# Mamba-2 scan and PReLU feed-forward on one core: weight conversion two pieces ahead with its add on GpSimd, states kept unmasked, first decays spread earlier

## The chip, the cores and the metric

The kernel runs on 1 core of one Trainium2 chip. The metric is the device time of one execution, in microseconds (us); lower is better. A core has TensorE (PE in the profile, with its weight loads as PEld), VectorE (DVE), ScalarE (ACT), GpSimd (POOL) and SyncE (SP), which here only issues DMAs. Each engine works through its own instructions in order; they meet at semaphores.

## The reference

Two blocks follow each other. The first is a chunked state-space scan over 4 batches x 8 heads x 768 positions, head size 32, state size 16; the second a feed-forward block over the 3072 tokens, 256 -> 2048 -> 256, with a slope alpha for each hidden unit.

```python
log_a = np.log(np.clip(a, 1e-06, 1.0))
for c in range(nc):
    cum = np.cumsum(la, axis=-1)
    L = np.exp(cum[:, :, :, None] - cum[:, :, None, :]) * causal
    M = np.einsum('bhin,bhjn->bhij', Cc, Bc) * L
    y_intra = np.einsum('bhij,bhjd->bhid', M, xc)
    y_inter = np.einsum('bhin,bhnd->bhid', Cc, state) * np.exp(cum)[:, :, :, None]
    y[:, :, sl] = y_intra + y_inter
    state = decay_full * state + sum_j(Bc_j x_j * decay_from_j)
# (batch, head, seq, dim) -> (batch*seq, head*dim)
h = x @ w_in
out = (np.maximum(h, 0.0) + alpha * np.minimum(h, 0.0)) @ w_out
```

x, a, B and C are float32. w_in and w_out come as float64, 8 bytes a number, so the kernel has to turn them into float32 itself.

## The kernel before

**Scan.** The sequence is cut into 24 chunks of 128 positions (Q), two chunks at a time as a "pair" (`pair`, L264): pairs 0 to 11, three to a batch. `pair` is a Python generator, and each `ssm(gp)` emits its next stage, so the author places the stages by hand between the matmuls of the feed-forward block. The stages are: (1) `rows_prep` for pairs 0 and 6, clamps of the broadcast decays `abc` on POOL (L272), `bn` (B times the decay to the chunk's end) on POOL (L279), the prefix products `pf` on DVE (L285, L288), four transposes of B and C on PE (L296), and on ACT the copies `bh` and the four scaled `cz` (L300, L303); (2) the decay matrix `dec` of the first chunk, and `cd` (L325); (3) `dec` of the second chunk, then the chunk's contribution to the state: a matmul `dps` (L333), its product with the block mask `bmask` (`dm`, L335), and the running `state` (L345); (4), (5) for each chunk the products C*B on PE (L356), multiplied into `dec` on DVE (L361); (6) the output `y` on PE, from the state (L370) and from `dec` (L377), copied by ACT into `xT` (L383), the input of the feed-forward block.

`dec` is a scan over 1024 columns. For pairs 2 and up its input is `abc`, a DMA that broadcasts decays to all partitions (L115). For pairs 0 and 1 there is no such DMA: PE spreads the rows with 16 small matmuls a chunk (two PSUM tiles, L318), and DVE scans each tile of 512 columns (L322). The mask is needed because all 8 heads share the 128 state partitions: head h's 16 rows may only meet its own 32 columns.

**Weights.** 16 pieces of 512 KB (8 of w_in for two hidden blocks each, 8 of w_out for two blocks each). `load_weights` (L142) issues the DMA into one of six `raw` buffers. `convert_a` (L152) makes two parts on ACT (L163, L166). `convert` (L169) finishes on DVE: sign bits (L184, or L187 twice for w_out, with the sign of the slope), a clamp (L190), shift and xor (L192), and an integer add of the rounded low part (L195), which writes the piece into `w_in` or `w_out`.

**Feed-forward.** `hidden` (L390): two k-steps of matmuls into one of two PSUM buffers `hp` (L396), then ACT multiplies by the slope (L399) and DVE takes the larger or smaller of the two (L400). `output` (L403) runs 2 hidden blocks later (LAG) and accumulates into `po` (L409).

**Order.** PE, DVE and ACT run in the order in which the code emits (`manual_schedule`, L43); for POOL and SP a planner orders the instructions, so a load may be issued well before its place in the code. Token group 0 (512 tokens, pairs 0 and 1) is worked in two halves: n=0 runs 16 hidden blocks on pair 0's 256 tokens, n=1 on pair 1's, with outputs from f=2 on. The loop (L445) converts piece i+1 at odd f, right after `hidden(f)`, and loads piece i+6 at even f. `first` and `second` name the f at which stages of pairs 1, 2 and 3 are emitted. From group 1 on, blocks are 512 tokens wide and pair stages are placed at fixed f.

Of the kernel before, what the change touches and what calls it, by code (L numbers as in the profile page):

```python
# [9 lines left out]
F32 = mybir.dt.float32  # L10
U32 = mybir.dt.uint32
# [11 lines left out]
def kernel(  # L23
# [20 lines left out]
        mybir.EngineType.PE, mybir.EngineType.DVE, mybir.EngineType.Activation}))  # L44
# [3 lines left out]
    P = 128  # L48
# [120 lines left out]
    def convert(dst, src, sg):  # L169

        d = dst.bitcast(U32)
        sg = sg()
        if src.dtype == F32:
            for i in range(2 if sg else 0):
                nc.vector.tensor_scalar(out=d[:, i], in0=d[:, i], scalar1=sg[i], scalar2=None,
                                        op0=ALU.bitwise_xor)
            return
        hi, t, g = parts.pop(id(dst))  # L180
        tf = t.bitcast(F32)
        r = wtp.tile([P, 2, WQ], U32, name="wr")
        if sg is None:
            nc.vector.tensor_single_scalar(out=r, in_=hi, scalar=SIGN, op=ALU.bitwise_and)  # L184
        else:
            for i in range(2):
                nc.vector.tensor_scalar(out=r[:, i], in0=hi[:, i], scalar1=SIGN, scalar2=sg[i],  # L187
                                        op0=ALU.bitwise_and, op1=ALU.bitwise_xor)
# [6 lines left out]
        nc.vector.tensor_tensor(out=d, in0=r, in1=g.bitcast(U32), op=ALU.add)  # L195
# [25 lines left out]
    alp = ps_s.tile([P, 512], F32, name="ss")  # L221
    nc.tensor.transpose(alp[:, :NF], al_n, ident[:NF, :NF])
    over = const.tile([P, NF], F32, name="over")
    nc.vector.tensor_scalar(out=over, in0=alp[:, :NF], scalar1=1.0, scalar2=None, op0=ALU.is_gt)
    s_mul = const.tile([P, NF], F32, name="s_mul")
    nc.vector.tensor_scalar(out=s_mul, in0=over, scalar1=-2.0, scalar2=1.0, op0=ALU.mult,
                            op1=ALU.add)
    s_alpha = const.tile([P, NF], F32, name="s_alpha")
    nc.vector.tensor_tensor(out=s_alpha, in0=alp[:, :NF], in1=s_mul, op=ALU.mult)
    s_out = const.tile([P, NF], U32, name="s_out")  # L230
    nc.vector.tensor_single_scalar(out=s_out, in_=s_mul.bitcast(U32), scalar=SIGN,
                                   op=ALU.bitwise_and)
# [4 lines left out]

    prt = {}
    firsts = {}

    def rows_prep(i):
# [5 lines left out]
        if i == 0:  # L247
            z = prep.tile([RW, Q], F32, name="z0")
            nc.vector.tensor_scalar(out=z, in0=rows, scalar1=1e-6, scalar2=1.0,
                                    op0=ALU.max, op1=ALU.min)  # L250
            nc.vector.memset(z[:, :1], 0.0)
            firsts[0] = z
# [11 lines left out]
    def pair(gp):  # L264

        b, c = divmod(2 * gp, CPB)
        nat, abc, xt, ap = loads.pop(("p", gp))
        last = c + 2 == CPB
        if gp % 6 == 0:
            rows_prep(gp // 6)  # L270
        for t in abc:
# [10 lines left out]
            in1=pj.unsqueeze(3).to_broadcast([P, 2, H, N]), op=ALU.mult)  # L282

# [6 lines left out]


# [12 lines left out]
        cd = work.tile([P, 2, Q], F32, name="cd")  # L304
        yield


        dec = work.tile([P, 2, H, Q], F32, name="dec")
        dv = dec.rearrange("p k h t -> p k (h t)")
        for k in range(2):  # L310
            if abc:
                nc.vector.tensor_tensor_scan(out=dv[:, k], data0=abc[k], data1=ident_h,  # L312
                                             initial=0.0, op0=ALU.mult, op1=ALU.add)
            for w in range(0 if abc else 2):
                t = ps_s.tile([P, 512], F32, name="ss")
                for q in range(4):
                    row = (b % 2 * H + 4 * w + q) * CPB + c + k
                    nc.tensor.matmul(t[:, q * Q : (q + 1) * Q],  # L318
                                     ident[:RW, row : row + 1].to_broadcast([RW, P]), firsts[0],
                                     start=(q == 0), stop=True, skip_group_check=True)  # L320
                ws = slice(512 * w, 512 * w + 512)
                nc.vector.tensor_tensor_scan(out=dv[:, k, ws], data0=t, data1=ident_h[:, ws],  # L322
                                             initial=0.0, op0=ALU.mult, op1=ALU.add)
            if k == 0:
                nc.vector.tensor_tensor(out=cd.rearrange("p k t -> p (k t)"), in0=ct, in1=pf,  # L325
                                        op=ALU.mult)
                yield
# [4 lines left out]
        for k in range(nk):  # L332
            nc.tensor.matmul(dps[:, k * HD : (k + 1) * HD], bn[:, k], xt[:, k], start=True, stop=True)  # L333
        dm = work.tile([P, 2, HD], F32, name="dm")
        nc.vector.tensor_tensor(  # L335
            out=dm[:, :nk], in0=dps[:, : nk * HD].rearrange("p (k m) -> p k m", m=HD),
            in1=bmask.unsqueeze(1).to_broadcast([P, nk, HD]), op=ALU.mult)
        st = [state.get(b)]
        for k in range(nk):
            if st[k] is None:  # L340
                st.append(dm[:, k])
                continue
            new = work.tile([P, HD], F32, name=f"state{k}")
            e = (k + 1) * Q - 1
            nc.vector.scalar_tensor_tensor(out=new, in0=st[k], scalar=pf[:, e : e + 1],  # L345
                                           in1=dm[:, k], op0=ALU.mult, op1=ALU.add)
            st.append(new)
        state[b] = st[-1]
# [155 lines left out]
```

## Time and profile before

| | |
|---|---|
| median of 3 runs | 456.19 us (454.41 to 457.52) |
| the profiled execution | 456.93 us, span 455.2 us |
| PEld busy | 284.0 us (62%) |
| ACT busy | 124.3 us (27%) |
| POOL busy | 35.1 us (8%), 62 instructions |
| HBM read / written | 26.85 MB / 3.15 MB |

The span runs from the first to the last instruction of the profiled execution. "Busy" is the time in which an engine has an instruction running; matmuls are pipelined, and their ends are modelled. In the strips, each digit is the busy share of one of 40 equal slices, in tenths. An idle time is put down to whatever released the instruction that ended it, so a row `A <- B: 21.3, 8` says that A stood still 21.3 us in all, 8 times, until B was done.

### The profile page before, as it was taken

How to read it: one execution, taken by the hardware profiler on the slowest of the kernel's cores; microseconds unless marked ns; L12 is line 12 of the kernel's file. 1: busy time of each engine (PE TensorE's matmuls, PEld its weight loads, DVE VectorE, ACT ScalarE, POOL GpSimd, SP SyncE). 2: the span in 40 equal slices, each digit the busy share in tenths (PEclk: the TensorE clock that was granted, in tenths of full speed). 3: DMA queues.
4: the chain of work that ended last, by engine and by line, in shares of the span. 5: the costliest groups of instructions: out<-in, count | busy, mean ns of one | idle time of the engine just before them, and what ended most of it. 6: DMA issues, size and time to landing. Idle time of an engine off the chain costs nothing.

```text
span 455.2 us, 4968 instructions
## 1 busy us (share of the span) xinstructions
PE 421.7 (93%) x1931; PEld 284.0 (62%) x1931; DVE 230.6 (51%) x354; ACT 124.3 (27%) x229; POOL 35.1 (8%) x62
## 2 busy tenths in 40 slices
PE   3875755999999999999999999999999999999996
PEld 3564543787865665665765766666666666666664
DVE  4859676789575174283273273283283372122121
ACT  3133442543231231241231231311321311131121
POOL 2021002002001001012011021020010000000000
PEclk9959787999999999999999999999999999999999
DMA  9989473441151141161150170130020000010001
GB/s 176 240 219 177 120 170 110 117 79 47 24 121 54 23 88 40 23 135 40 24 120 7 24 170 3 24 93 1 0 94 0 0 1 0 1 47 0 1 0 46
DMA packets 105207, 30.31 MB, mean 67 GB/s; under 512 B 75792, under 2 KB 101088, under 8 KB 105184
## 3 DMA queue, kind: packets, MB, share of 16 engines
q1 hardware_dynamic: 101024, 29.74, 27.9%
q10 hardware_dynamic: 4160, 0.26, 0.7%
q8 instruction: 15, 0.25, 0.2%
q14 instruction: 8, 0.07, 0.0%
HBM read 26.85 MB, written 3.15 MB: 66 GB/s over the span
## 4 chain that ended last, share of the span: by engine, by line
PE 86%; DVE 9%; DMA 1%; ACT 1%; issue 1%; ACTq 0%; DVEq 0%
PE hp L396 37%; PE po L409 36%; PE ss L356 5%; PE ss L377 2%; PE ss L370 2%; PE ss L318 1%; PE ss L333 1%; DVE wr L192 1%; DMA nat<-in_C_dram 1%; DVE dec L322 1%; DVE gt L400 1%; DVE w_in L195 1%; DVE dec L312 1%; PE ss L296 1%; ACT gt L399 1%
## 5 line engine op out<-in xcount | busy, mean ns | idle before, releaser
L396 PE MATMUL hp<-xT,w_in 128*128 128x512 f32 (+1 forms) x448 | 192.4, 556 | 22.1 <-DVE w_in L195 21.3
L409 PE MATMUL po<-w_out,gt 128*128 128x256 f32 x768 | 181.1, 379 | 0.0
L409 PEld LDWEIGHTS po<-w_out,gt 128*128 128x128 f32 x768 | 145.9, 190 | 54.0 <-issue 38.3
L400 DVE SCALAR_TENSOR_TENSOR gt<-hp,s_mul,gt 128x512 f32<-128x512 f32 (+1 forms) x112 | 75.3, 673 | 186.9 <-ACT gt L399 186.0
L399 ACT ACTIVATE gt<-hp,s_alpha 128x512 f32<-128x512 f32 (+1 forms) x112 | 70.4, 629 | 263.7 <-PE hp L396 263.7
L396 PEld LDWEIGHTS hp<-xT,w_in 128*128 128x128 f32 x448 | 84.5, 198 | 89.3 <-issue 52.2
L312 DVE TENSOR_TENSOR_SCAN dec<-abc,ident_h 128x1024 f32<-128x1024 f32 x20 | 46.0, 2300 | 0.0
L361 DVE TENSOR_TENSOR dec<-ss,dec 128x512 f32<-128x512 f32 x48 | 30.8, 685 | 18.5 <-PE ss L356 18.5
L272 POOL TENSOR_SCALAR abc<-abc 128x1024 f32<-128x1024 f32 x20 | 21.3, 1066 | 180.4 <-DMA abc<-in_a_dram 118.2
L356 PE MATMUL ss<-cz,bh 64*128 64x512 f32 x96 | 29.4, 682 | 0.0
L303 ACT ACTIVATE cz<-ss,par 128x256 f32<-128x256 f32 x48 | 18.9, 482 | 0.0
L279 POOL TENSOR_TENSOR bn<-nat,prt 128x256 f32<-128x256 f32 x12 | 9.2, 773 | 120.4 <-PE ss L333 72.2
L383 ACT COPY xT<-ss 128x512 f32<-128x512 f32 x12 | 7.0, 586 | 36.3 <-PE ss L377 36.3
L356 PEld LDWEIGHTS ss<-cz,bh 64*128 64x128 f32 x96 | 7.9, 195 | 9.2 <-issue 7.6
L377 PE MATMUL ss<-dec,xt 128*32 128x128 f32 x384 | 13.3, 276 | 0.2 <-DVE dec L361 0.2
L322 DVE TENSOR_TENSOR_SCAN dec<-ss,ident_h 128x512 f32<-128x512 f32 x8 | 9.6, 1215 | 5.2 <-PE ss L318 5.2
L318 PEld LDWEIGHTS ss<-z,ident 96*128 96x128 f32 x64 | 11.4, 274 | 0.2
L192 DVE SCALAR_TENSOR_TENSOR wr<-wt,wr 128x512 uint32<-128x512 uint32 x16 | 11.1, 692 | 0.5
L318 PE MATMUL ss<-z,ident 96*128 96x128 f32 x64 | 11.3, 356 | 0.0
L333 PE MATMUL ss<-xt,bn 128*128 128x256 f32 x40 | 11.1, 392 | 0.0
L377 PEld LDWEIGHTS ss<-dec,xt 128*32 128x32 f32 x384 | 9.6, 109 | 2.1 <-DVE dec L361 0.6
L166 ACT ACTIVATE wg<-raw 128x512 f32<-128x512 uint16 x16 | 10.8, 674 | 0.0
(51 smaller groups left out, 142.5 us busy)
## 6 DMA issues: line engine op xcount, KB each, us to landing
abc<-in_a_dram SPq DMA_DIRECT2D x20, 512.0 KB, 3.7
raw<-in_moe_w_in_dram SPq DMA_DIRECT2D x8, 512.0 KB, 6.6
raw<-in_moe_w_out_dram SPq DMA_DIRECT2D x8, 512.0 KB, 3.4
xt<-in_x_dram SPq DMA_DIRECT2D x24, 128.0 KB, 3.8
out_dram<-o_sb SPq DMA_DIRECT2D x12, 256.0 KB, 2.6
ap<-in_a_dram SPq DMA_DIRECT2D x12, 128.0 KB
nat<-in_B_dram SPq DMA_DIRECT2D x22, 64.0 KB, 2.9
nat<-in_C_dram SPq DMA_DIRECT2D x22, 64.0 KB, 2.8
```

What stands on the lines that cost most here:

```text
L192: nc.vector.scalar_tensor_tensor(out=r, in0=t, scalar=3, in1=r, op0=ALU.logical_shift_left, op1=ALU.bitwise_xor)
L272: nc.gpsimd.tensor_scalar(out=t, in0=t, scalar1=1.0, scalar2=1e-6, op0=ALU.min, op1=ALU.max)
L303: nc.scalar.mul(cz[:, e].rearrange("p k t -> p (k t)"), ct, par[:, e : e + 1])
L312: nc.vector.tensor_tensor_scan(out=dv[:, k], data0=abc[k], data1=ident_h, initial=0.0, op0=ALU.mult, op1=ALU.add)
L318: nc.tensor.matmul(t[:, q * Q : (q + 1) * Q], ident[:RW, row : row + 1].to_broadcast([RW, P]), firsts[0], start=(q == 0), stop=True, skip_ ...
L356: nc.tensor.matmul(gram[r].rearrange("p h t -> p (h t)"), bh[rs, k], cz[rs, :, k], start=True, stop=True, tile_position=(64 * r, 0), skip_ ...
L361: nc.vector.tensor_tensor(out=dec[:, k, hs], in0=gram[r], in1=dec[:, k, hs], op=ALU.mult)
L377: nc.tensor.matmul(y[32 * q : 32 * q + 32, w, k], xt[:, k, h * D : (h + 1) * D], dec[:, k, h], start=False, stop=True, tile_position=(0, 3 ...
L396: nc.tensor.matmul(hp, w_in[:, k, f * P : (f + 1) * P], xts[g][:, k, t0 : t0 + nt], start=(k == 0), stop=(k == KC - 1))
L399: nc.scalar.mul(gt, hp, s_alpha[:, f : f + 1])
L400: nc.vector.scalar_tensor_tensor(out=gt, in0=hp, scalar=s_mul[:, f : f + 1], in1=gt, op0=ALU.mult, op1=ALU.max)
L409: nc.tensor.matmul(pos[g][t // 2][:, t % 2], gt[:, t * Q : (t + 1) * Q], w_out[:, f], start=(f == 0 and t % 2 == 0), stop=(f == NF - 1), s ...
```

## The change

Six things change.

- POOL also runs in the order in which the code emits.
- The integer add of a weight conversion (L195) is done by POOL instead of DVE.
- Pieces 0 and 1 are both converted ahead of the loop, and in the loop piece i+2 is converted at even f (its ACT part ahead of `hidden(f)`, the rest behind it). Piece 2 is loaded ahead of pair 1. The stages of pairs 1, 2 and 3 have new places: pair 2's decays and C*B products move from the first half into the second.
- The state is kept unmasked: the update reads `dps` from PSUM itself, and the first chunk of a batch is copied by ACT. POOL makes a masked copy `sm` for the two chunks, which only the matmul of L370 reads.
- Pair 0's first two spreading tiles are emitted right after the rows are clamped (`rows_first`), ahead of `rows_prep`, the slopes (now in `slopes`) and the pair's transposes; its first decays are scanned before the clamps and `pf`, the second two tiles before the transposes. Its six stages are placed between the conversions of pieces 0 and 1.
- `cd` moves to the end of the first stage.

```diff
     ctx.enter_context(tc.manual_schedule(engines={
-        mybir.EngineType.PE, mybir.EngineType.DVE, mybir.EngineType.Activation}))
+        mybir.EngineType.PE, mybir.EngineType.DVE, mybir.EngineType.Activation,
+        mybir.EngineType.Pool}))
...
-        nc.vector.tensor_tensor(out=d, in0=r, in1=g.bitcast(U32), op=ALU.add)
+        nc.gpsimd.tensor_tensor(out=d, in0=r, in1=g.bitcast(U32), op=ALU.add)
...
+    def rows_first():
+
+        z = prep.tile([RW, Q], F32, name="z0")
+        nc.vector.tensor_scalar(out=z, in0=loads["r", 0], scalar1=1e-6, scalar2=1.0,
+                                op0=ALU.max, op1=ALU.min)
+        nc.vector.memset(z[:, :1], 0.0)
+        firsts[0] = z
...
+    def spread(b, c, w):
+
+        t = ps_s.tile([P, 512], F32, name="ss")
+        for q in range(4):
+            row = (b % 2 * H + 4 * w + q) * CPB + c
+            nc.tensor.matmul(t[:, q * Q : (q + 1) * Q],
+                             ident[:RW, row : row + 1].to_broadcast([RW, P]), firsts[0],
+                             start=(q == 0), stop=True, skip_group_check=True)
+        return t
...
+        def decays(k):
+
+            if abc:
+                nc.vector.tensor_tensor_scan(out=dv[:, k], data0=abc[k], data1=ident_h,
+                                             initial=0.0, op0=ALU.mult, op1=ALU.add)
+                return
+            for w in range(2):
+                t = ahead.pop(0) if ahead else spread(b, c + k, w)
+                ws = slice(512 * w, 512 * w + 512)
+                nc.vector.tensor_tensor_scan(out=dv[:, k, ws], data0=t, data1=ident_h[:, ws],
+                                             initial=0.0, op0=ALU.mult, op1=ALU.add)
+
+        ahead = []
+        if gp == 0:
+            rows_first()
+            ahead = [spread(b, c, w) for w in range(2)]
+            rows_prep(0)
+            slopes()
+            decays(0)
+        elif gp == 6:
+            rows_prep(1)
+        bn = pair_loads(gp)
...
+        if gp == 0:
+            decays(1)
...
+        nc.vector.tensor_tensor(out=cd.rearrange("p k t -> p (k t)"), in0=ct, in1=pf, op=ALU.mult)
         yield
...
+        if gp:
+            decays(0)
+            yield
+            decays(1)
...
-        dm = work.tile([P, 2, HD], F32, name="dm")
-        nc.vector.tensor_tensor(
-            out=dm[:, :nk], in0=dps[:, : nk * HD].rearrange("p (k m) -> p k m", m=HD),
-            in1=bmask.unsqueeze(1).to_broadcast([P, nk, HD]), op=ALU.mult)
-        st = [state.get(b)]
+        st = [masked.get(b)]
+        new = work.tile([P, 2, HD], F32, name="state")
         for k in range(nk):
...
+            old = state.get(b)
+            if old is None:
+                nc.scalar.copy(out=new[:, k], in_=dps[:, k * HD : (k + 1) * HD])
+            else:
+                e = (k + 1) * Q - 1
+                nc.vector.scalar_tensor_tensor(out=new[:, k], in0=old, scalar=pf[:, e : e + 1],
+                                               in1=dps[:, k * HD : (k + 1) * HD],
+                                               op0=ALU.mult, op1=ALU.add)
+            state[b] = new[:, k]
+        sm = work.tile([P, 2, HD], F32, name="sm")
+        nc.gpsimd.tensor_tensor(out=sm[:, :nk], in0=new[:, :nk],
+                                in1=bmask.unsqueeze(1).to_broadcast([P, nk, HD]), op=ALU.mult)
+        st += [sm[:, k] for k in range(nk)]
+        masked[b] = st[-1]
         yield
...
-    for i in range(2):
+    for i in range(3):
         load_weights(*pieces[i])
     load_pair(1)
-    for i in range(2, 6):
+    for i in range(3, 6):
         load_weights(*pieces[i])
-    ssm(0, 5)
+    ssm(0)
     convert_a(*pieces[0])
+    ssm(0)
     convert(*pieces[0])
+    ssm(0, 2)
     convert_a(*pieces[1])
     ssm(0)
     load_pair(2)
-
-    first = {2: (1, 1), 3: (1, 1), 4: (1, 1), 6: (1, 1), 8: (1, 1), 10: (1, 1),
-             11: (2, 1), 12: (2, 1), 13: (2, 1), 15: (2, 1)}
-    second = {1: (2, 1), 3: (2, 1), 4: (3, 1), 6: (3, 1), 7: (3, 1), 9: (3, 1), 11: (3, 1), 13: (3, 1)}
+    convert(*pieces[1])
+
+    first = {1: (1, 1), 4: (1, 1), 6: (1, 1), 8: (1, 1), 10: (1, 1), 12: (1, 1), 14: (2, 1)}
+    second = {0: (2, 1), 1: (2, 1), 2: (2, 1), 3: (2, 1), 5: (2, 1), 6: (3, 1), 7: (3, 1),
+              8: (3, 1), 9: (3, 1), 11: (3, 1), 13: (3, 1)}
...
+            if f % 2 == 0 and i + 2 < len(pieces):
+                convert_a(*pieces[i + 2])
             hidden(0, f, n * 2 * Q, 2 * Q)
-            if f % 2 == 0 and i + 6 < len(pieces):
-                load_weights(*pieces[i + 6])
-            if f % 2 == 1 and i + 1 < len(pieces):
-                convert(*pieces[i + 1])
+            if f % 2 == 0:
+                if i + 6 < len(pieces):
+                    load_weights(*pieces[i + 6])
                 if i + 2 < len(pieces):
-                    convert_a(*pieces[i + 2])
+                    convert(*pieces[i + 2])
```

More of the change, by code (lines that the diff above doesn't have):

```diff
@@ L218, with slopes @@
     nc.vector.memset(ends[:, Q - 1 :], 1.0)
[L221 to L224, printed above, removed]
     s_mul = const.tile([P, NF], F32, name="s_mul")
[L226 to L227 removed]
     s_alpha = const.tile([P, NF], F32, name="s_alpha")
[L229 removed]
     s_out = const.tile([P, NF], U32, name="s_out")
[L231 to L232 removed]
+    def slopes():
+        alp = ps_s.tile([P, 512], F32, name="ss")
+        nc.tensor.transpose(alp[:, :NF], al_n, ident[:NF, :NF])
+        over = const.tile([P, NF], F32, name="over")
+        nc.vector.tensor_scalar(out=over, in0=alp[:, :NF], scalar1=1.0, scalar2=None,
+                                op0=ALU.is_gt)
+        nc.vector.tensor_scalar(out=s_mul, in0=over, scalar1=-2.0, scalar2=1.0, op0=ALU.mult,
+                                op1=ALU.add)
+        nc.vector.tensor_tensor(out=s_alpha, in0=alp[:, :NF], in1=s_mul, op=ALU.mult)
+        nc.vector.tensor_single_scalar(out=s_out, in_=s_mul.bitcast(U32), scalar=SIGN,
+                                       op=ALU.bitwise_and)
     xts = {}
     state = {}
+    masked = {}
     prt = {}
     firsts = {}
+    def rows_first():
[4 more added lines that the diff above has]
+        firsts[0] = z
     def rows_prep(i):
@@ L262, in rows_prep, with pair_loads @@
         prt[i] = t
-    def pair(gp):
+    def pair_loads(gp):
         b, c = divmod(2 * gp, CPB)
[L267 to L270, printed above, removed]
+        nat, abc, xt, ap = loads["p", gp]
         for t in abc:
@@ L282, in pair @@
             in1=pj.unsqueeze(3).to_broadcast([P, 2, H, N]), op=ALU.mult)
+        return bn
+    def spread(b, c, w):
[6 more added lines that the diff above has]
+        return t
+    def pair(gp):
+        b, c = divmod(2 * gp, CPB)
+        nat, abc, xt, ap = loads["p", gp]
+        last = c + 2 == CPB
+        dec = work.tile([P, 2, H, Q], F32, name="dec")
+        dv = dec.rearrange("p k h t -> p k (h t)")
+        def decays(k):
[18 more added lines that the diff above has]
+        bn = pair_loads(gp)
         pf = work.tile([P, 2 * Q], F32, name="pf")
@@ L304, in pair @@
         cd = work.tile([P, 2, Q], F32, name="cd")
+        nc.vector.tensor_tensor(out=cd.rearrange("p k t -> p (k t)"), in0=ct, in1=pf, op=ALU.mult)
         yield
[L308 to L327, printed above, removed]
+        if gp:
+            decays(0)
+            yield
+            decays(1)
         nk = 1 if last else 2
```

15 lines of the change are left out of this document (removed).

## The prediction

> **What bounds the kernel now.** I read the page first, then busy time by stage, then the waits and the chain inside the stage that stood out.
>
> ```profile
> span 455.2 us, 4968 instructions
> ...
> PE 421.7 (93%) x1931; PEld 284.0 (62%) x1931; DVE 230.6 (51%) x354; ACT 124.3 (27%) x229; POOL 35.1 (8%) x62
> ...
> PE   3875755999999999999999999999999999999996
> ...
> DMA  9989473441151141161150170130020000010001
> ```
> ```profile
> 22.09:80.50 58.41, 39.02 (x170) 27.04 (x170) 41.18 (x72) 20.81 (x44) 8.13 (x13) 0.77 0.68 157
> ...
> 87.13:150.00 62.87, 62.87 (x297) 47.19 (x294) 42.79 (x73) 21.77 (x43) 5.55 (x9) 1.00 0.31 68
> 150.00:440.00 290.00, 289.48 (x1284) 187.46 (x1283) 123.82 (x162) 70.92 (x124) 17.79 (x28) 1.00 0.16 38
> ```
>
> The second fence gives, for each stretch, its length, then the busy time of PE, PEld, DVE, ACT and POOL, the granted clock, and DMA. From 87 us on PE is never idle, so nothing on DVE or POOL can shorten that part. The first half of token group 0 (22.09, first hidden matmul, to 80.50) is different: PE is busy 39.0 of 58.4 us, and at a granted clock of 0.77. The waits of that part name one cause above all, and the chain of waits shows its shape:
>
> ```profile
> PE hp L396 <- DVE w_in L195: 21.3, 8, 5.3
> ```
> ```profile
> 54.43 0.48 DVE gt L400
> 54.91 0.34 DVE wr L184
> ...
> 56.45 0.70 DVE w_in L195
> ...
> 57.20 1.15 PE hp L396 x4
> ```
>
> VectorE finishes the activation of one hidden block, only then converts the next weight piece (54.91 to 57.15, all of it serial), and the next hidden matmul starts the moment its piece is written. PE lost 21.3 us in 8 such waits. DVE itself was busy only 41.2 of the 58.4 us, so that stage is a chain through several engines, not a full DVE.
>
> **The change part by part.** Its worth is the shift of the point from which PE is never idle. I follow the new order to the start of the hidden matmul of f=3, second half, which was at 87.2 before; what follows it is unchanged PE work.
>
> ```profile
> 85.30 0.89 PE ss L370 x8
> 86.19 1.01 PE ss L377 x32
> 87.20 1.06 PE hp L396 x4
> ```
>
> *Remainder.* From 87.1 to 455.2 are 368.1 us. The new lists put pair 2's last stage (L370, L377) at f=5 instead of f=3, so 0.89 + 1.01 = 1.9 us move behind this point: 370.0 us remain.
>
> *Conversion two pieces ahead.* At f even, piece i+2 is converted, and it is used four hidden blocks later, not in the next one. The wait of L396 for L195 goes. What is late next: the hidden matmul of f needs the PSUM buffer of f-2 (two buffers), so it waits for the DVE activation of f-2. Between that and its own activation lie one matmul group (1.06), ACT (about 0.5) and hand-offs; DVE has the conversion and the activation of f-1 to do meanwhile (about 2 us), so I expect DVE to run nearly without gaps, and its sum sets the stage. The rows for it, mean ns of one (the second fence has min/median/max):
>
> ```profile
> L312 DVE TENSOR_TENSOR_SCAN dec<-abc,ident_h 128x1024 f32<-128x1024 f32 x20 | 46.0, 2300 | 0.0
> L361 DVE TENSOR_TENSOR dec<-ss,dec 128x512 f32<-128x512 f32 x48 | 30.8, 685 | 18.5 <-PE ss L356 18.5
> L400 DVE SCALAR_TENSOR_TENSOR gt<-hp,s_mul,gt 128x256 f32<-128x256 f32 x32 | 15.3, 481 | 23.2 <-ACT gt L399 23.1
> ...
> L288 DVE TENSOR_TENSOR_SCAN pf<-ap,zeros 128x128 f32<-128x128 f32 x24 | 9.6, 443 | 0.4
> L322 DVE TENSOR_TENSOR_SCAN dec<-ss,ident_h 128x512 f32<-128x512 f32 x8 | 9.6, 1215 | 5.2 <-PE ss L318 5.2
> ...
> L187 DVE TENSOR_SCALAR wr<-raw,s_out 128x256 uint32<-128x256 uint32 x16 | 5.3, 370 | 0.0
> L325 DVE TENSOR_TENSOR cd<-ss,pf 128x256 f32<-128x256 f32 x12 | 4.8, 398 | 0.0
> ...
> L285 DVE TENSOR_SCALAR ap<-ap 128x256 f32<-128x256 f32 x12 | 3.4, 284 | 0.0
> ```
> ```profile
> L345 DVE SCALAR_TENSOR_TENSOR state<-state,pf,dm x12: 484/485/1353, 40.7 to 369.5; 128x256 f32<-128x256 f32 x12
> ...
> L184 DVE TENSOR_SCALAR wr<-raw x8: 416/419/868, 19.6 to 70.4; 128x512 uint32<-128x512 uint32 x8
> ```
>
> A conversion without its add is the chain's 54.91 to 56.45 = 1.54; for w_out pieces, with two L187 of 0.37, about 1.75. First half, f=0 to 15: 16 activations 7.7; pieces 2 to 7, 9.2; pieces 8 and 9, 3.5; pair 1: clamp, two pf scans and cd 1.6, four L322 4.9, two states 1.0, four L361 2.7; pair 2's first stage 1.6. Sum 32.2. Second half up to the activation of f=1, which frees the buffer of f=3: two L312 4.6, two activations 1.0, piece 10 1.75, one state 0.5. Sum 7.8. Together 40.0 us. PE's own work in the first half fits beside it: 16 x 1.06 of hidden matmuls and less than 10 us of pair 1.
>
> *Add on POOL.* It takes 0.70 a piece off DVE. The trace has no integer add there; nearest is bn below, 0.64 for 256 columns of two inputs, so 1.28 for 512. Bounds: half of the 1024-column clamp, 0.52, and the longest bn, 1.90. I take 1.28, the like operation. Behind the add on POOL's queue, now in written order, stand bn, the mask of pair 1 and, at f=14, pair 2's two clamps. None is needed within 4 us, and the piece itself has four blocks' time, so it costs PE nothing while the sum stays under some 8 us.
>
> ```profile
> L279 POOL TENSOR_TENSOR bn<-nat,prt x12: 638/664/1895, 6.9 to 304.4; 128x256 f32<-128x256 f32 x12
> ```
> ```profile
> 17.23 2.48 DVE L361 TENSOR_TENSOR dec<-ss,dec 128x512 f32<-128x512 f32 x4
> ...
> 66.45 0.64 POOL L279 TENSOR_TENSOR bn<-nat,prt 128x256 f32<-128x256 f32 x1 [20.63 <-PE ss L333]
> 66.57 2.67 DVE L312 TENSOR_TENSOR_SCAN dec<-abc,ident_h 128x1024 f32<-128x1024 f32 x1
> ...
> 69.88 1.10 POOL L272 TENSOR_SCALAR abc<-abc 128x1024 f32<-128x1024 f32 x1 [2.79 <-DMA abc<-in_a_dram]
> ...
> 70.38 0.87 DVE L184 TENSOR_SCALAR wr<-raw 128x512 uint32<-128x512 uint32 x1
> ```
>
> But POOL and DVE get in each other's way: the L312 scan took 2.67 instead of 2.30 beside a bn, and L184 0.87 instead of its median 0.42 beside a clamp. L312 and the conversion's operations read only SBUF. An activation reads PSUM (hp) and follows each conversion, so most of the add falls beside harmless work: about 0.4 us is left over per piece where no pair stage lies between, more at f=1, f=6 and f=14; I count 4 us. Against it, means overstate back-to-back work: four L361 in a row took 2.48, 0.62 each and not 0.69, and some 70 operations at an estimated 0.06 give 4 us back. The two cancel, and both ends stay in the range (0 to 4 less, 0 to 14 more).
>
> The Trainium skill speaks against this edit (GPSIMD Engine Reference, Engine selection and Specifications): it keeps two-input elementwise work on VectorE and says that GpSimd's SBUF interfaces are shared with VectorE operations of two SBUF inputs or of a two-port mode. The rows above agree with the sharing. By its 2.6 cycles an element at 1.2 GHz an add would be an estimated 1.1 us, and by the sharing the rival below holds.
>
> *Masked copy by POOL.* L335 (a product from PSUM) leaves DVE; the state update reads PSUM and SBUF, 0.49 as before. For a batch's first chunk ACT copies instead. The mask, 1.28 by bn's rate, has three stages to the L370 that reads it: nothing, as long as POOL keeps up.
>
> *Spreading moved up, and the start.* The start decides when the 40 us begin.
>
> ```profile
> 3.38 0.06 DVE L218 MEMSET ends<- 128x1 f32 x1
> ...
> 5.44 0.42 PE L259 MATMUL ss<-ident,pr 96*128 96x96 f32 x1 [1.61 <-DVE pr L255]
> ...
> 9.28 1.57 ACT L303 ACTIVATE cz<-ss,par 128x256 f32<-128x256 f32 x4
> 10.71 0.69 ACT L163 ACTIVATE wt<-raw 128x512 f32<-128x512 f32 x1
> 10.72 1.22 DVE L322 TENSOR_TENSOR_SCAN dec<-ss,ident_h 128x512 f32<-128x512 f32 x1 [3.54 <-PE ss L318]
> ...
> 12.43 1.22 DVE L322 TENSOR_TENSOR_SCAN dec<-ss,ident_h 128x512 f32<-128x512 f32 x1 [0.48 <-PE ss L318]
> ...
> 22.09 2.62 PE L396 MATMUL hp<-xT,w_in 128*128 128x256 f32 x8 [1.90 <-DVE w_in L195]
> ```
>
> z is ready at about 3.8 (L218 ends at 3.44, then 0.2 and 0.06), the two spreads cost 12.43 - 10.72 = 1.71 each while PE is cold: 7.3. The transposes of rows (0.42) and slopes follow on PE, and DVE's copy and four small slope operations wait for them, an estimated 1.0 more: 8.7. Two scans, 11.1; pf, 12.2; the second two spreads wait for the first two buffers (9.9 and 11.1), so PE ends them near 12.4 and only then starts the four nat transposes (13.1). Two more scans and cd: DVE 14.9. ACT copies (0.4) and scales (1.57) until 15, converts piece 0 (two of 0.69, overlapped) until 16.2, copies the first state 16.6; DVE updates the state until 17.1, and now piece 0's conversion and the mask share the port: 19.6. Four L361 (2.48) end at 22.1; the last matmuls and the xT copy take an estimated 1.1 more (half an L377 group and one ACT copy): hidden starts at 23.2, 1.1 later than before. ACT has piece 2's two activations (1.2) ahead of the first gt, so DVE's first activation starts at 24.8.
>
> *Loads.* Piece 2 goes ahead of pair 1; DMA is above 80% in the first 45 us, and SP's order later is open.
>
> ```profile
> 39.31 0.96 SPq L147 DMA_DIRECT2D raw<-in_moe_w_out_dram  x1
> ...
> 47.14 8.55 SPq L147 DMA_DIRECT2D raw<-in_moe_w_out_dram  x3
> ```
>
> Piece 8 was issued at 39.3 and 9 to 11 from 47.1, part of it waiting for buffers that now come free sooner. They are wanted at about 49, 54 and 58: no cost if they keep these times.
>
> *Sum.* 24.8 + 40.0 = 64.8 for the hidden matmul of f=3; 64.8 + 370.0 = 434.8 for the span. The profiled execution took 456.93 for its span of 455.2 (+1.7), and the median of the runs is 456.19, 0.7 lower: 435.8, so **436 us**, 4.4% less.
>
> **The rivals.**
> *Port conflict takes it back.* If every add and mask of the stage stops DVE (10 x 1.28 + 1.9 = 14.7 instead of 4): about 447. For it: the two slowed rows; against: activations and gram products read PSUM.
> *Weights late.* If pieces 9 and 10 are issued at the end of the 8.55 us, 55.7, and land some 3.5 later, the loop waits about 5 us: 441; another few for a worse order, 445. For it: a saturated queue; against: buffers free sooner.
> *No gain.* Everything holds, but the stage was DMA's anyway: then hidden blocks go on at the old pace, from a start 1.1 later: 457. Against: the waits name L195, not a transfer.
> *Slower.* The integer add is slow on POOL. With p us each it stops DVE or PE's next piece for 10 x (p - 1.28); faster turns into slower by over 1% when this passes 20.2 + 4.6 us, p = 3.8, twice the longest bn; at p = 4.5 it would be 468. No row shows an integer add, so it can't be excluded.
>
> **How the numbers follow.** Chances: forecast 0.60 (its own range 431 to 442), port conflict 0.15, weights late 0.09, no gain 0.08, slower 0.08. The range of 431 to 448 leaves out the last two: 431 is the sum with 4 us of overlap and no conflict, 448 the conflict in full. Within 1% (451.6 to 460.8), about what a measurement of this kernel can tell from no change, I give 0.09 (no gain, and the conflict's upper end); slower by more 0.08; faster 0.83.
>
> **What would show it.** Right: L396's wait for a weight piece gone from the waits of the first 70 us, replaced by waits for L400; POOL adds near 1.28; the first hidden matmul near 23 and PE without gaps from about 65; some DVE conversions lengthened beside POOL's work. Wrong: adds of 3 us or more, conversions of 2 us and above, ACT waiting for raw's DMA, or a first hidden matmul later than 26.

## The result, and the profile after

The changed kernel takes 444.24 us (median of 4 runs, 443.12 to 445.43), the kernel before 456.61 us beside it: a ratio of 0.9736, with a 95% interval of 0.9692 to 0.978. That is 2.6% faster; 436 us had been forecast, in a range of 431 to 448.

The page of the changed kernel, its first lines and the strip of PE:

```profile
span 442.5 us, 4977 instructions
...
PE 422.9 (96%) x1931; PEld 285.4 (64%) x1931; DVE 216.7 (49%) x326; ACT 125.2 (28%) x233; POOL 70.3 (16%) x90
...
PE   6779969999999999999999999999999999999996
```

PE's work is what it was (421.7 before, 422.9 now); only idle time has gone, and POOL's work has doubled (35.1 to 70.3). Busy time by stage, columns as in the prediction, for the first activation on DVE to the hidden matmul of f=3, second half, and from there on:

```profile
25.36:72.38 47.02, 38.92 (x181) 27.05 (x179) 42.08 (x71) 22.18 (x47) 18.94 (x17) 0.82 0.81 199
72.38:150.00 77.62, 77.62 (x412) 57.82 (x413) 43.15 (x72) 25.14 (x51) 19.73 (x23) 1.00 0.29 62
```

The hidden matmul of f=3 starts at 72.3 instead of 87.1 us. PE's last gap ends 8.8 us ahead of it; in the kernel before, it ended 4.7 us ahead. Here are that wait before and after, and the stretch from there in the changed kernel, which is full of PE work at a granted clock of 0.67:

```profile
82.44 1.13 PE L396 MATMUL hp<-xT,w_in 128*128 128x256 f32 x4 [0.81 <-DVE gt L400]
```
```profile
63.55 2.08 PE L431 MATMUL hp<-xT,w_in 128*128 128x256 f32 x4 [0.78 <-DVE gt L435]
```
```profile
63.55:72.38 8.83, 8.83 (x25) 4.89 (x25) 8.80 (x11) 2.06 (x4) 4.58 (x3) 0.67 0.70 152
```

DVE is busy 42.1 of the 47.0 us between its first activation and f=3. The waits of this stage (A <- B, us in all, times, longest) have changed their name:

```profile
PE hp L431 <- DVE gt L435: 8.1, 7, 2.6
```
```profile
DVE gt L435 <- ACT gt L434: 5.3, 4, 2.6
```

No hidden matmul waits for a weight piece any more. PE waits 8.1 us for activations on DVE where it waited 21.3 us for conversions. Of DVE's 5.3 us, 2.6 lie ahead of its first activation, so 2.8 lie inside the 47.0 us. The timeline of the stage shows what fills DVE (start, length, idle time in front in brackets):

```profile
22.77 2.04 PE L431 MATMUL hp<-xT,w_in 128*128 128x256 f32 x4 [0.78 <-ACT xT L418]
...
24.85 0.47 ACT L434 ACTIVATE gt<-hp,s_alpha 128x256 f32<-128x256 f32 x1 [1.11 <-PE hp L431]
...
25.36 0.48 DVE L435 SCALAR_TENSOR_TENSOR gt<-hp,s_mul,gt 128x256 f32<-128x256 f32 x1 [2.57 <-ACT gt L434]
...
27.38 1.28 POOL L196 TENSOR_TENSOR w_in<-wr,wg 128x512 uint32<-128x512 uint32 x1 [3.17 <-DVE wr L193]
...
27.48 2.17 DVE L334 TENSOR_TENSOR_SCAN pf<-ap,zeros 128x128 f32<-128x128 f32 x2
...
33.34 1.22 DVE L316 TENSOR_TENSOR_SCAN dec<-ss,ident_h 128x512 f32<-128x512 f32 x1 [0.52 <-PE ss L294]
...
42.11 1.27 POOL L380 TENSOR_TENSOR sm<-state,bmask 128x512 f32<-128x512 f32 x1 [2.19 <-DVE state L375]
...
42.34 1.32 DVE L185 TENSOR_SCALAR wr<-raw 128x512 uint32<-128x512 uint32 x1
...
48.98 1.29 DVE L396 TENSOR_TENSOR dec<-ss,dec 128x512 f32<-128x512 f32 x2 [0.48 <-PE ss L391]
...
54.97 0.48 DVE L435 SCALAR_TENSOR_TENSOR gt<-hp,s_mul,gt 128x256 f32<-128x256 f32 x1 [2.13 <-ACT gt L434]
...
57.35 1.26 DVE L331 TENSOR_SCALAR ap<-ap 128x256 f32<-128x256 f32 x1
...
58.54 1.04 POOL L276 TENSOR_SCALAR abc<-abc 128x1024 f32<-128x1024 f32 x1
...
58.65 1.53 DVE L334 TENSOR_TENSOR_SCAN pf<-ap,zeros 128x128 f32<-128x128 f32 x2
...
61.04 0.99 DVE L188 TENSOR_SCALAR wr<-raw,s_out 128x256 uint32<-128x256 uint32 x2
...
63.24 1.27 POOL L196 TENSOR_TENSOR w_out<-wr,wg 128x512 uint32<-128x512 uint32 x1 [1.35 <-DVE wr L193]
...
63.41 3.25 DVE L310 TENSOR_TENSOR_SCAN dec<-abc,ident_h 128x1024 f32<-128x1024 f32 x1
...
68.53 2.28 DVE L310 TENSOR_TENSOR_SCAN dec<-abc,ident_h 128x1024 f32<-128x1024 f32 x1
...
68.76 3.13 POOL L196 TENSOR_TENSOR w_out<-wr,wg 128x512 uint32<-128x512 uint32 x1 [4.25 <-DVE wr L193]
...
72.31 1.13 PE L431 MATMUL hp<-xT,w_in 128*128 128x256 f32 x4
```

Six DVE rows are longer than the same work alone: L334 2.17 and 1.53 (two scans took 0.74 in the kernel before), L185 1.32 (0.42), L331 1.26 (0.28), L188 0.99 (0.61) and L310 3.25 (2.28). Together that is 5.4 us, each beside a POOL instruction. At 68.5 it is the other way round: the scan was first, and the add takes 3.13 instead of 1.28.

### The profile page after: what moved, and what is told of

Same layout as the page of the kernel before. It is cut to its first block, busy times and chain, and to the rows that moved or that the text cites. A ratio compares the mean times of both kernels' runs of the same rounds, so it can differ in the third digit from the quotient of the medians.

```text
span 442.5 us, 4977 instructions
## 1 busy us (share of the span) xinstructions
PE 422.9 (96%) x1931; PEld 285.4 (64%) x1931; DVE 216.7 (49%) x326; ACT 125.2 (28%) x233; POOL 70.3 (16%) x90
## 4 chain that ended last, share of the span: by engine, by line
PE 86%; DVE 5%; SPq 3%; DMA 3%; issue 1%; ACT 1%; ACTq 0%; DVEq 0%
PE po L444 37%; PE hp L431 37%; PE ss L391 5%; DMA nat<-in_C_dram 3%; PE ss L412 3%; PE ss L405 2%; SPq L111 2%; PE ss L366 1%; SPq L109 1%; PE ss L344 1%; DVE gt L435 1%; DVE pf L334 1%; DVE wr L193 1%; DVE dec L316 1%; DVE wr L185 0%
## 5 line engine op out<-in xcount | busy, mean ns | idle before, releaser
L434 ACT ACTIVATE gt<-hp,s_alpha 128x512 f32<-128x512 f32 (+1 forms) x112 | 70.3, 629 | 241.6 <-PE hp L431 241.4
L310 DVE TENSOR_TENSOR_SCAN dec<-abc,ident_h 128x1024 f32<-128x1024 f32 x20 | 47.2, 2362 | 0.0
L380 POOL TENSOR_TENSOR sm<-state,bmask 128x512 f32<-128x512 f32 (+1 forms) x12 | 13.1, 1095 | 212.7 <-DVE state L375 212.7
L396 DVE TENSOR_TENSOR dec<-ss,dec 128x512 f32<-128x512 f32 x48 | 30.8, 685 | 21.4 <-PE ss L391 21.4
L391 PE MATMUL ss<-cz,bh 64*128 64x512 f32 x96 | 29.8, 682 | 0.2 <-ACT cz L351 0.2
L196 POOL TENSOR_TENSOR w_out<-wr,wg 128x512 uint32<-128x512 uint32 x8 | 13.9, 1739 | 23.4 <-DVE wr L193 20.7
L418 ACT COPY xT<-ss 128x512 f32<-128x512 f32 x12 | 7.0, 585 | 35.1 <-PE ss L412 35.1
L294 PE MATMUL ss<-z,ident 96*128 96x128 f32 x64 | 12.9, 384 | 4.0 <-DVE r L260 3.9
L294 PEld LDWEIGHTS ss<-z,ident 96*128 96x128 f32 x64 | 12.2, 290 | 4.2 <-POOL zeros L216 3.8
L391 PEld LDWEIGHTS ss<-cz,bh 64*128 64x128 f32 x96 | 8.0, 196 | 10.1 <-issue 7.8
L196 POOL TENSOR_TENSOR w_in<-wr,wg 128x512 uint32<-128x512 uint32 x8 | 10.2, 1276 | 21.5 <-DVE wr L193 16.7
L405 PEld LDWEIGHTS ss<-cd,sm 128*128 128x128 f32 x80 | 10.7, 191 | 3.4 <-issue 2.8
L405 PE MATMUL ss<-cd,sm 128*128 128x128 f32 x80 | 10.9, 276 | 2.0 <-DVE dec L396 2.0
L334 DVE TENSOR_TENSOR_SCAN pf<-ap,zeros 128x128 f32<-128x128 f32 x24 | 11.9, 536 | 0.5
```

Of the source, the lines that this page charges most:

```text
L196: nc.gpsimd.tensor_tensor(out=d, in0=r, in1=g.bitcast(U32), op=ALU.add)
L294: nc.tensor.matmul(t[:, q * Q : (q + 1) * Q], ident[:RW, row : row + 1].to_broadcast([RW, P]), firsts[0], start=(q == 0), stop=True, skip_ ...
L391: nc.tensor.matmul(gram[r].rearrange("p h t -> p (h t)"), bh[rs, k], cz[rs, :, k], start=True, stop=True, tile_position=(64 * r, 0), skip_ ...
L396: nc.vector.tensor_tensor(out=dec[:, k, hs], in0=gram[r], in1=dec[:, k, hs], op=ALU.mult)
L405: nc.tensor.matmul(y[:, w, k], st[k][:, w * P : (w + 1) * P], cd[:, k], start=not begun, stop=False, skip_group_check=True)
L434: nc.scalar.mul(gt, hp, s_alpha[:, f : f + 1])
```

## The experiments

All times stand beside runs of the kernel before on the same chip; the ratio and its 95% interval are what is compared. Line numbers differ a little from kernel to kernel; the names stay. "f=3" stands for the start of the hidden matmul of f=3 in the second half, 72.3 us in the changed kernel. The last two columns are of one profiled execution each. There the first matmul group takes 1.1 us in some kernels and 2.0 to 2.1 in others, as the granted clock has it (1.10 at 1.00 in e7, 2.04 at 0.50 in the changed kernel, with nearly the same start), so a difference of under a microsecond at the start says little.

| kernel | us | ratio | interval | first hidden | f=3 |
|---|---|---|---|---|---|
| changed | 444.24 | 0.9736 | 0.9692 to 0.978 | 22.8 | 72.3 |
| e8: order alone | 464.84 | 1.0188 | 1.0115 to 1.0261 | 22.8 | 88.5 |
| e1: add on DVE | 471.1 | 1.0313 | 1.0244 to 1.0382 | 24.2 | 92.9 |
| e9: add on DVE, split | 452.33 | 0.9916 | 0.9887 to 0.9945 | 24.6 | 75.8 |
| e11: order alone, add split | 445.87 | 0.9772 | 0.9745 to 0.9799 | 21.5 | 71.3 |
| e2: mask on DVE | 441.5 | 0.9671 | 0.9613 to 0.9729 | 21.3 | 70.2 |
| e3: spreading as before | 444.16 | 0.9734 | 0.9686 to 0.9783 | 23.3 | 72.0 |
| e5: ACT's part later | 443.12 | 0.9724 | 0.9687 to 0.9761 | 22.9 | 70.7 |
| e10: e2 and e5 | 440.07 | 0.9653 | 0.9624 to 0.9682 | 21.3 | 69.4 |
| e7: add twice | 447.2 | 0.9817 | 0.9786 to 0.9849 | 22.7 | 75.1 |
| e12: clamps earlier | 443.26 | 0.9712 | 0.9669 to 0.9756 | 23.1 | 73.4 |
| e6: PE kept busy | 444.3 | 0.975 | 0.9722 to 0.9779 | 23.2 | 72.5 |
| e14: e10 and e12 | 441.19 | 0.9681 | 0.9641 to 0.9722 | 21.3 | 69.9 |

### Is it the order, or the work taken off DVE?

My theory was that the order brings the gain (the wait for the next piece goes) and that DVE's sum then sets the stage, so that the add is worth its own time on DVE, less what POOL's sharing takes back. The rival was that DVE's relief is the gain. Two kernels were to tell them apart. e8 is the kernel before with the new loop, the new lists of stages and piece 2 loaded first, and nothing else of the change.

> The kernel before with the new order alone: pieces two ahead, the new places of the pair stages, piece 2 loaded ahead of pair 1. Add, mask and spreading as before. If the order is what brings the gain (the wait of the hidden matmul for its weight piece goes, DVE's sum sets the stage), DVE pays nine adds of about 0.6 and two masks more than in the changed kernel, but is not stopped by POOL: 445 to 449 us, the hidden matmul of f=3 of the second half near 75. If the gain comes from taking work off DVE, this stays near the kernel before: 453 to 457.

e1 is the changed kernel with one word undone:

```diff
-        nc.gpsimd.tensor_tensor(out=d, in0=r, in1=g.bitcast(U32), op=ALU.add)
+        nc.vector.tensor_tensor(out=d, in0=r, in1=g.bitcast(U32), op=ALU.add)
```

> The changed kernel with the integer add back on DVE. My reading: of the 5.4 us by which POOL lengthens DVE rows in the first stage, about 3.3 stand beside adds; they go, and nine adds of 0.6 come: 2 us slower than the changed kernel, 446 us. Rival, the port takes all of it back: no difference, 444, or faster. Rival, the port does not matter: 5 us slower, 449 to 450.

Both fell outside everything expected. e8 took 464.84 us and e1 471.1 us: both slower than the kernel before, e1 by 27 us against the changed kernel, far more than nine adds of 0.7. The waits of e1's first 120 us and its PE timeline:

```profile
PE hp L431 <- DVE w_in L196: 18.0, 6, 5.2
```
```profile
24.23 2.08 PE L431 MATMUL hp<-xT,w_in 128*128 128x256 f32 x4 [0.70 <-ACT xT L418]
26.09 1.06 PE L344 MATMUL ss<-ident,nat 128*128 128x128 f32 x4
26.95 1.06 PE L431 MATMUL hp<-xT,w_in 128*128 128x256 f32 x2
29.61 3.38 PE L431 MATMUL hp<-xT,w_in 128*128 128x256 f32 x8 [1.60 <-DVE w_in L196]
```
```profile
28.86 0.69 DVE L196 CUSTOM_DVE_ANT_0 w_in<-wr,wg 128x1024 uint16<-128x1024 uint16 x1
```

The hidden block of f=1 needs four rows, two for each k step. Its first k step runs at 26.95; its second stops until 29.61, when DVE has written piece 2 (the add at 28.86), which that block does not read (it reads piece 0). The program's own list of waits says the same. In e1 the second k step of f=1 waits for DVE, in the changed kernel it waits for nothing:

```
e1       L431 MATMUL hp_337<-xT_277,w_in_116 128x256
         L431 MATMUL hp_337<-xT_277,w_in_116 128x256 [waits DVE_49]
changed  L431 MATMUL hp_337<-xT_277,w_in_116 128x256 x2
```

A w_in piece is 256 columns in each of two k blocks, 2048 columns apart. My new theory: DVE's add, which the program holds as its own custom instruction with an output of 2 x 512 halves, is recorded as writing all columns from the first block's start to the second's end, and the second k step of every block up to that piece reads inside that span; POOL's ordinary add is recorded block by block. So converting ahead on DVE makes PE wait for the newest piece. The recording itself is not seen, only its waits: in e1's list the second k steps of f=1, 3 and 5 wait for pieces 2, 3 and 4, and the first k steps, which read outside the span, wait for no piece that is converted ahead. e9 tests the theory with the add on DVE, as one add for each k block:

```diff
-        nc.gpsimd.tensor_tensor(out=d, in0=r, in1=g.bitcast(U32), op=ALU.add)
+        for i in range(2):
+            nc.vector.tensor_tensor(out=d[:, i], in0=r[:, i], in1=g[:, i].bitcast(U32), op=ALU.add)
```

> The changed kernel with the add on DVE, as in e1, but as two adds, one for each k block of the piece. In e1 the second k step of a hidden matmul waited for the newest conversion, which it does not read: DVE's one add is recorded as writing all columns between the two k blocks. If that recorded dependence is what made e1 slow, it goes here, and only DVE's own time is left: nine conversions longer by 0.7 to 0.9, some 3.3 us of POOL's stops less: 446 to 449 us, no wait of L432 for the adds of pieces ahead. Rival, e1 was slow because DVE cannot carry the adds: 463 or more again.

e11 does the same to e8.

> The kernel before with the new order alone, as in e8, and the add on DVE as two adds, one for each k block. With the recorded dependence gone the order alone, with all work left on DVE, should give most of the gain: 446 to 451 us. Rival, the order is worth nothing unless work leaves DVE: 460 or more again.

e9 took 452.33 us, 19 us less than e1, and e11 445.87 us, 19 us less than e8, though each has more DVE instructions than its partner (by the ratios to the kernel before, 18 and 19 us). In their lists the second k step of f=1 waits for nothing, and PE's wait for w_in is gone from both; e9's PE waits for DVE's activations instead:

```profile
PE hp L432 <- DVE gt L436: 9.7, 7, 3.9
```

So the recorded dependence accounts for 18 to 19 us in both pairs. And e11, with the mask, the spreading and the adds on DVE, lies within the interval of the changed kernel (0.9772 against 0.9692 to 0.978): the order alone, once PE need not wait for columns that it does not read, brings most of the gain. Its f=3 is even 1.0 us earlier than the changed kernel's, but from there to the end it takes 372.7 us instead of 370.2, because PE still waits for activations behind f=3 (2.2 us, twice). e9 missed its 446 to 449 by 3 us. It differs from e11 by the masked copy on POOL, the early spreading, the first stage's `cd` and POOL's written order, starts 3.1 us later (24.6 against 21.5) and ends 6.5 us later; which of these does it was not taken apart. With everything else equal, the add on POOL rather than split on DVE is worth 8 us (444.24 against 452.33).

### The masked copy and the spreading

e2 puts the mask back on DVE (the product L335 and the update from SBUF, as in the kernel before) and drops `sm`.

> The changed kernel with the masked state as before (the masking product on DVE, the update from SBUF), no masked copy on POOL. My reading: two stops by the masked copy go (1.1 at the start on the clamp of piece 0, 0.9 on the sign bits near 42 us), two products of 0.67 come: within 1 us of the changed kernel, 444 to 445. Rival, the copy on POOL is a clear gain: 446 or more.

It took 441.5 us, 2.7 us less than the changed kernel rather than the same, though the intervals overlap. The timeline of e2's PE shows the first hidden matmul 1.5 us and the one of f=3 2.2 us earlier (the first two lines). The gain lies at the start. There the changed kernel's masked product stops the clamp of piece 0, 1.50 us instead of 0.42 (the last two lines, of the changed kernel). DVE's first activation is 2.4 us earlier in e2 (22.92; 0.9 of this is a first matmul group at full clock), and from it to f=3 e2 takes 47.2 us, no less than the changed kernel's 47.0:

```profile
21.27 1.10 PE L429 MATMUL hp<-xT,w_in 128*128 128x256 f32 x4 [0.80 <-ACT xT L416]
```
```profile
70.15 1.13 PE L429 MATMUL hp<-xT,w_in 128*128 128x256 f32 x4 [0.31 <-DVE gt L433]
```
```profile
16.67 1.32 POOL L380 TENSOR_TENSOR sm<-state,bmask 128x512 f32<-128x512 f32 x1 [7.88 <-DVE state L375]
16.78 1.50 DVE L191 TENSOR_SCALAR wt<-wt 128x512 f32<-128x512 f32 x1
```

e3 puts pair 0's spreading and scans back behind slopes, clamps and transposes.

> The changed kernel with pair 0's spreading and scans where they were (behind the slopes, the clamps and the transposes). The four scans ended at 16.2 before and end at 14.6 now, so the first hidden matmul comes about 1.6 us later, 24.4, and the time is 445 to 446. Rival, the start is set elsewhere (transposes, ACT): the same first hidden matmul, 22.8, and 444.

The first hidden matmul comes at 23.3 instead of 22.8, 0.5 us later and not 1.6, and the time is the changed kernel's (444.16). The early spreading brings the first hidden matmul forward by half a microsecond, and no gain from it shows at the end. In e3's profile the first group runs at full clock, so its first activation is even 0.45 us earlier (24.91); what the half microsecond is worth at an equal clock is not shown.

### What holds the rest of the stage

Three causes were on the table for the time that the forecast missed: POOL stopping DVE, ACT's parts standing ahead of the activation, and the lowered clock. e7 doubles the first (every POOL add is done twice).

> The changed kernel with every POOL add done twice (the same sum, written again): 1.28 us more of POOL for each piece, nothing else. If POOL's adds cost DVE time through the shared port, ten pieces of the first stage cost up to 1.28 each, at half of them about 6: 448 to 453 us, with more lengthened DVE rows. If an add is hidden as long as its piece is in time: 444 to 445.

It took 447.2 us, 3.0 more, just under the 448 to 453 expected. DVE's rows in the stage show where most of it goes, the changed kernel's first, then e7's:

```profile
L334 DVE TENSOR_TENSOR_SCAN pf<-ap,zeros 128x128 f32<-128x128 f32 x4 | 3.7, 964 | 0.1
L185 DVE TENSOR_SCALAR wr<-raw 128x512 uint32<-128x512 uint32 x6 | 3.4, 568 | 0.0
```
```profile
L185 DVE TENSOR_SCALAR wr<-raw 128x512 uint32<-128x512 uint32 x6 | 5.9, 982 | 0.0
...
L335 DVE TENSOR_TENSOR_SCAN pf<-ap,zeros 128x128 f32<-128x128 f32 x4 | 5.4, 1383 | 0.1
```

With the clamps and the sign bits of w_out (0.4 and 0.8 us more) DVE's rows are about 5.4 us longer, some 0.6 for each of the nine added adds of 1.28: the sharing costs, but about half of an add stands beside work that it does not disturb. PE also waits 1.8 us, three times, for a second add to end. About 3 us of all this reach the end, 0.3 for each add.

e12 was to take one group of stops away: pair 2's two clamps on POOL are emitted at f=5, not at f=14.

```diff
+            if n == 0 and f == 5:
+                clamps(2)
             if f in (first, second)[n]:
```

> The changed kernel with POOL's two clamps of pair 2's decays emitted at f=5 instead of f=14, beside scans that read PSUM. At 57 to 61 us they and one add stop DVE for about 2.1 us (clamp of ap 1.0, pf 0.8, sign bits 0.4). If those stops lie on the path: 441.5 to 443 us, and the hidden matmul of f=3 in the second half 1.5 to 2 us earlier than 72.4. If the time moves to another wait: 444.

It took 443.26 us, with an interval that holds the changed kernel's ratio, and f=3 is not earlier (73.4). But the edit removed few stops. Behind the early clamps POOL's masked copy starts later, and now stops a clamp of DVE (1.49 us instead of 0.42) where it stopped the sign bits before, and `bn` stops the `pf` scans. DVE's rows are still lengthened by about 4.8 us in all, against 5.4. DVE also waits more for ACT: 7.0 us where it was 5.3 (2.9 and 2.6 of it ahead of the first activation). Whether the stops lie on the path stays open.

```profile
44.23 1.42 POOL L385 TENSOR_TENSOR sm<-state,bmask 128x512 f32<-128x512 f32 x1
44.44 1.49 DVE L191 TENSOR_SCALAR wt<-wt 128x512 f32<-128x512 f32 x1
```
```profile
DVE gt L440 <- ACT gt L439: 7.0, 5, 2.9
```

e5 moves ACT's part of a conversion from in front of the hidden matmul of even f to behind that of odd f.

```diff
-            if f % 2 == 0 and i + 2 < len(pieces):
-                convert_a(*pieces[i + 2])
             hidden(0, f, n * 2 * Q, 2 * Q)
...
+            if f % 2 == 1 and i + 3 < len(pieces):
+                convert_a(*pieces[i + 3])
             if n and f >= LAG:
```

> The changed kernel with ACT's part of piece i+3 emitted behind the hidden matmul of odd f, not ahead of that of even f. If the missing time in the first stage is DVE waiting for ACT (2.6 us at the first block, 2.1 near 55 us), it shrinks: first activation on DVE near 24 instead of 25.4, 441 to 443 us. Rival, only POOL's stops of DVE matter: 444, the time moves elsewhere.

It took 443.12 us, 1.1 less and within the interval: not told from no change, though f=3 starts 1.6 us earlier in its profile. Of the two waits that it was aimed at, the one near 55 us shrinks from 2.13 to 1.32. The one at the first block does not (2.70 after 2.57), because there ACT itself waits for PE's first matmul group, which takes 2.04 us:

```profile
24.98 0.47 ACT L434 ACTIVATE gt<-hp,s_alpha 128x256 f32<-128x256 f32 x1 [2.23 <-PE hp L431]
```

e6 keeps PE busy, by doing the first matmul of each hidden block of the first half twice (the second overwrites the first).

> The changed kernel with the first matmul of each hidden block of the first half done twice (overwritten by the second), 16 x 0.43 = 6.9 us more of PE, to keep PE busy while it waits. If the lowered clock (0.81 granted in that stage, matmul groups of 2.08 instead of 1.06) makes DVE wait, the clock goes above 0.9 and the time falls or stays: 442 to 444.5. If the clock does not matter there, each block only gets 0.43 longer before ACT and DVE: 445 to 448.

It took 444.3 us, inside the first range and below the second. The clock granted between 22.8 and 72.4 us rose from 0.81 in the changed kernel (first line) to 0.94:

```profile
22.77:72.38 49.61, 41.51 (x187) 29.18 (x187) 42.10 (x72) 23.63 (x50) 20.21 (x18) 0.81 0.82 194
```
```profile
22.77:72.38 49.61, 43.13 (x218) 32.10 (x218) 41.68 (x71) 24.30 (x51) 19.81 (x18) 0.94 0.82 193
```

This does not settle what the clock is worth. The added matmuls are 6.9 us at full clock, but PE's busy time in the stretch rose by only 1.6 us (41.5 to 43.1), since all its matmuls there ran faster. The longer first block delays DVE's first activation by 1.25 us (26.61), and the way from there to f=3 is 1.1 us shorter (45.9): gain and added work cancel. At f=3 at least the clock is not the limit. There PE, now faster, waits for DVE's state:

```profile
71.41 1.12 PE L391 MATMUL ss<-cz,bh 64*128 64x512 f32 x2 [0.25 <-DVE state L375]
```

Two kernels put the helpful ones together: e10 (mask on DVE, ACT's part later) and e14 (e10 and the early clamps).

> The mask back on DVE (as in e2, 441.5) and ACT's part late (as in e5). If the two act on different waits, their gains add: 438.5 to 440.5. If both only move the same wait: 441 to 442.

> Mask back on DVE, ACT's part late (e10, 440.1) and the early clamps of e12 together. If the clamps' stops add to the rest: 438 to 439. If not: 440.

e10 took 440.07 us; its interval, 0.9624 to 0.9682, lies wholly below the changed kernel's. It is the fastest here, 3.5% below the kernel before and 0.9% below the change (440.07 / 444.24). It differs from e5 by the mask alone, and e5's interval, 0.9687 to 0.9761, lies wholly above e10's: with ACT's part late, the mask on DVE is worth 3.0 us, clear of the noise. What ACT's later part adds to e2 (441.5) is not clear of it. The early clamps add nothing to e10: 441.19, with an interval that holds e10's ratio.

## Why the prediction was right, point by point

- **The direction and the stage**: right. PE's work after f=3 was to take 370.0 us and took 442.5 - 72.3 = 370.2, so the whole difference lies in front of it. But 444.24 lies outside the 431 to 442 that the prediction gave the forecast itself, and inside its range only through the part kept for the port conflict, which did not come in full. That the time fell into the range is partly luck.
- **The start**: right to 0.6 us. First hidden matmul 23.2 forecast, 22.77 measured; first activation on DVE 24.8 against 25.36. The mask and piece 0's conversion do get in each other's way there, as said, and e2 shows the price: without the masked copy the first hidden matmul is at 21.3. The last step came out for another reason than forecast. ACT's two parts of piece 2 end at 23.7 and hold nothing up; the first activation waits for PE's first group, which took 2.04 us instead of 1.06 (the row at 24.85).
- **The loop, 40.0 us forecast, 47.0 measured** (25.36 to 72.31): this is the term that was mis-sized, and it makes 7.0 of the 7.5 us by which f=3 came late. Its parts: the sum of rows less the saving of back-to-back work was 36, and DVE's 42.08 busy less 5.4 of stops is 36.7; stops were put at 4 and are 5.4; idle time of DVE was put at none and is 47.0 - 42.1 = 4.9. So the step that failed is "I expect DVE to run nearly without gaps". Of the gaps 4.3 us are six waits: 2.1 at 54.97, where ACT has xT's copy and a piece's two parts ahead of an activation; two of 0.3 for other activations; and three of 0.5 for PE's products, two of them for pair 1's spreading (L294) and one for C*B (L391). The rest are pauses of under 0.1 us between rows. The prediction's own check of this point compared the latency of one block with the work in between, and left out what ACT does ahead of the activation and what DVE needs from PE for the pair. What it would take to win the gaps back was not settled: moving ACT's parts (e5) is not told from no change, e12 removed few stops, and e6 leaves the clock's share open.
- **The add on POOL, 1.28 us**: right, 1.28 in every undisturbed row of the stage (the one of 3.13 stands behind a scan). That it costs PE nothing is not quite so: doubled, it costs about 0.3 us a piece.
- **What the add's move is worth**: wrong, though the total hides it. The prediction gave it 0.70 us a piece. With the add on DVE, and the new order, the kernel takes 471 us: the move is worth 27 us, 18 to 19 of them by the recorded dependence that it removes and that two smaller adds on DVE remove as well (e9). The step "The wait of L396 for L195 goes" was argued from the order and held only because the add left DVE, as e8 shows: that is luck. Every row that it rested on was of the kernel before, where the newest piece was also the one needed, so the two could not be told apart there.
- **The masked copy, "nothing, as long as POOL keeps up"**: wrong. Leaving it out gave 2.7 us with overlapping intervals (e2), and 3.0 us clear of them where ACT's part is late (e10 against e5).
- **The rivals**: port conflict in part (5.4 of the 14.7 us that it would take in full), weights late not seen, since no wait for a transfer shows up among PE's, DVE's or ACT's waits of the stage; no gain and slower are ruled out by the time and by adds of 1.28.

The Trainium skill's rule that POOL and DVE share SBUF interfaces (GPSIMD Engine Reference, Specifications) agrees with the lengthened rows here, in both directions (an L310 scan 3.25 us, an add 3.13). The Trainium skill's advice to keep two-input elementwise work on VectorE (GPSIMD Engine Reference, Engine selection) agrees with the masked copy here, where e10 beats e5 by 3.0 us. It does not agree with the add: on DVE, in two parts, it makes the changed kernel 8 us slower (e9), though e11 with all of it on DVE is as fast as the changed kernel within the noise.

## What to carry to other kernels

Before work is moved ahead in a schedule, look at which columns the next engine is made to wait for: an instruction that writes two distant blocks may be recorded as writing everything in between, and then being early makes the reader late. Splitting such a write into one instruction for each block costs a little time and can be worth far more (18 to 19 us here). When a chain becomes a sum, the sum of rows is a lower bound; allow for the gaps of the engines in front (here 10% of the stage) and for GpSimd's stops (another 13% of DVE's busy time).

## What the runs showed of the hardware

- In the changed kernel's trace DVE and POOL stop each other by turns: where both work on SBUF alone, the one that starts first keeps its length, and the other ends about when the first is done and its own length has passed. The L310 scan at 63.41 takes 3.25 us instead of 2.28 behind an add that ends at 64.51; the add at 68.76 takes 3.13 instead of 1.28 behind a scan that ends at 70.81. DVE's work that reads PSUM kept its length beside POOL: the activations of the stage average 0.478 us (0.481 before).
- POOL's 32-bit integer add of 512 columns takes 1.27 to 1.28 us where nothing stops it, the same as its float product with the mask (1.27 to 1.32). DVE's add of the same columns, on 1024 halves, takes 0.69.
- One matmul more in each of 16 hidden blocks raised the granted clock of a stage of 50 us from 0.81 to 0.94 and PE's busy time there by only 1.6 us; the time stayed where it was (444.3 us).
